# P times V by half tiles of keys in four arrays of TensorE, with the scores of another pair between its two halves

## Chip and metric

The kernel runs on one core of a Trainium2 chip. The metric is the device time of one execution in microseconds. Five engines appear in the profile: TensorE (PE; its weight loads stand apart as PEld), VectorE (DVE), ScalarE (ACT), GpSimd (POOL) and SyncE (SP), whose queue issues the transfers.

## What is computed

Windowed causal attention with a linear bias, followed by a gated MLP whose gate mixes positions. There are 8 batches of 8 heads, 576 positions, head dimension 64; the MLP is 512 to 1024 to 512. In short:

```python
scores = scale * np.matmul(q, k.transpose(0, 1, 3, 2))
mask = (rel >= 0) & (rel < 128)                 # a query sees itself and 127 keys before it
scores = np.where(mask, scores + bias[None], -1000000000.0)
attn = softmax(scores)
x = np.matmul(attn, v)                          # heads joined: (8, 576, 512)
h = np.maximum(x @ w_in, 0.0)
u, v = (h[..., :512], h[..., 512:])
v_n = (v - mean(v)) / np.sqrt(var(v) + 1e-06)
v_s = np.einsum('ts,bsd->btd', w_spatial, v_n) + b_spatial[None, :, None]
out = (u * v_s) @ w_out
```

## The kernel before

Attention works on pairs of heads. A tile holds the 64 dims of the one head in partitions 0-63 and those of the other in 64-127. The 576 queries are cut into nine blocks of 64 (`NB`), and a block of queries i meets at most the key blocks i-2, i-1 and i, so that its scores are 64, 128 or 192 columns wide (`WIDTH`). The first batch runs by a path of its own (`raw_tile`, `raw_sums`, `raw_out`); for the 28 pairs of the other batches the stages are these:

- `products` (L620, matmul L632): the scores, f32 matmuls that take 64 dims by 64 columns. For odd blocks the two heads swap partitions (`j ^ odd`), so that even blocks use two of the four 64x64 arrays and odd blocks the other two. They go block 0, 1, ... 8.
- `softmax` (L636): VectorE adds the bias and takes the maximum (L645), ScalarE takes the exponential with a sum (L651).
- `scores` (L661): scaling, and a split into a high and a low f16 plane in `pq` (ScalarE L685, VectorE L690). Two transposing transfers bring it to `pts`, keys in partitions (L696): one for even blocks, one for odd.
- `attention` (L701): v is scaled and split into f16 `vh` and `vl`; then P times V (L751). A matmul takes all 128 keys of a tile and 64 dims of a head (`j`), and streams a window of one, two or four blocks of queries (`WINDOWS`). Each window is done three times: vh with the high plane, vh with the low one, vl with the high one. Blocks of a window that do not use some of the keys meet zeros. The results stand in two PSUM banks (`xps`, queries 0 to 255 and 256 to 575), from where ScalarE (L766) and VectorE (L770) bring them to `xt`.
- `gated` (L799): the MLP of a batch, with units v (L822, and L844 for the last 64 positions), u (L874), spatial mixing (L895) and output (L921), all on the full 128x128 array. A layer norm follows every v unit; its power -0.5 is one GpSimd instruction (L792).

`clear` (L597) zeroes `pq` once, by one GpSimd memset behind the first batch's path.

The order of the instructions on each engine is set by a planner (`Plan`): every step has an engine, a cost and a due time, and a list scheduler simulates the engines and emits the steps in the order in which they begin there. The costs of the attention steps are set by hand: `SCORES`, `VALUES`, and `BOTH` for the step in which P times V of one pair is followed at once by the scores of the pair two further on ("glued", 22 of the 28). The first six pairs have their scores alone, and six pairs (the first four and the last two) their values alone.

Of the kernel before, what the change touches and what calls it, by code (L numbers as in the profile page):

```python
# [12 lines left out]
F16 = mybir.dt.float16  # L13
# [179 lines left out]
def attn_gmlp_kernel(ctx, tc, qk, v, w_in, w_spT, b_sp, w_out, outT):  # L193
# [3 lines left out]
    nc = tc.nc  # L197
    B, H, D, _, S = qk.shape
    P = 2 * D
    NP = H // 2  # L200
# [7 lines left out]
    PSC = 4096.0  # L208
    VORDER = (0, 4, 1, 2, 3)
    W = 3 * D  # L210
    QSPLIT = 2 * P
    NB = S // D

    SWITCH = 190
    SCORES, VALUES, BOTH = 1760, 1670, 3230


    WOUT = (2, 4, 6, 8)
# [8 lines left out]
    VDUE = 8000  # L227

    const = ctx.enter_context(tc.tile_pool(name="const", bufs=1))
    work = ctx.enter_context(tc.tile_pool(name="work", bufs=2))  # L230
    ps = ctx.enter_context(tc.tile_pool(name="ps", bufs=1, space=PSUM))
    ctx.enter_context(tc.manual_schedule())
    plan = Plan()
# [6 lines left out]
    def fixed(shape, dtype, name):  # L240
        t = const.tile(shape, dtype, name=name)
        return Buf(lambda: t)

    def dve(n, fast=False):
        return 75 + n / (1.92 if fast else 0.96)
# [20 lines left out]
    r1 = fixed([P, S], F32R, "r1")  # L266
    r2 = fixed([P, S], F32R, "r2")
    l2 = fixed([P, DH], F32R, "l2")
    BLOCKS = [*range(0, NB, 2), *range(1, NB, 2)]
    EVENS = (NB + 1) // 2  # L270
    WIDTH = [min(i + 1, 3) * D for i in BLOCKS]
    prob = fixed([P, sum(WIDTH)], F32, "prob")
    PLANE = [2 * EVENS * P - P, 2 * (NB - EVENS) * P - P]
    BASE = [0, 2 * PLANE[0]]
    pq = fixed([P, 2 * sum(PLANE)], F16, "pq")
    stat = [fixed([P, 4, NB], F32, f"stat{i}") for i in range(2)]

    rstat = fixed([P, 2, 4, 2 * NP], F32, "rstat")
# [3 lines left out]
    def parts(b, a, z, step=P, key=()):  # L282

        return [(b, (*key, k)) for k in range(a // step, -(-z // step))]
# [309 lines left out]
            tail(xt, due + 1200)  # L594

    def clear():
        plan.add("POOL", 2500, 0, lambda: nc.gpsimd.memset(pq(), 0.0), (), parts(pq, 0, 2 * sum(PLANE), 64))  # L597


    WINDOWS = (((0, 4, 0, 0), (1, 2, 0, 128)),  # L600
               ((1, 2, 1, 0), (2, 4, 0, 0), (3, 2, 0, 128), (3, 1, 1, 256), (4, 1, 0, 256)))


    def places(k):
        i = BLOCKS[k]
        bank, c0 = ((0, 3 * P), (2, 3 * P), (0, 0), (2, 0), (0, W), (2, W), (1, 0), (3, 0), (1, W))[i]
        odd = i % 2
        return i, odd, bank, c0, sum(WIDTH[:k]), BASE[odd] + (0 if i < 2 else P + (i // 2 - 1) * 2 * P + odd * D), WIDTH[k]

    def queries(pts, j, a, kt, n, s):  # L610

        x = [BASE[o] + a * PLANE[o] + 2 * kt * P + s * P + (j ^ o) * D for o in range(2)]
        flat = pts().rearrange("p a b -> p (a b)")
        if n == 1:
            return flat[:, x[0]:x[0] + D]
        ap = flat[:, x[0]:x[0] + D]
        steps = [[x[1] - x[0], 2], [1, D]]
        return bass.AP(ap.tensor, ap.offset, [ap.ap[0], [P, 2], *steps] if n == 4 else [ap.ap[0], *steps])

    def products(raw):  # L620

        RAWS = [(raw, t) for t in range(NQ)]
        sc = [plan.buf(ps, "s", 4, [P, 512], F32) for _ in range(4)]
        flat = lambda k: sc[k]().rearrange("p a b -> p (a b)")

        def f():
            order = sorted(range(NB), key=lambda k: (BLOCKS[k] // 2, BLOCKS[k]))
            for k in order:
                i, odd, bank, c0, _, _, n = places(k)
                for j in range(2):  # L630
                    rows = slice((j ^ odd) * D, ((j ^ odd) + 1) * D)
                    nc.tensor.matmul(flat(bank)[rows, c0:c0 + n], raw()[j * D:(j + 1) * D, 0, i * D:(i + 1) * D],  # L632
                                     raw()[j * D:(j + 1) * D, 1, (i + 1) * D - n:(i + 1) * D], start=True, stop=True, skip_group_check=True)
        return f, RAWS, [(x, 0) for x in sc], flat

    def softmax(p, due, st, sc, flat):  # L636

        SM, NM, RC, TM = range(4)
        for k in range(NB):
            i, odd, bank, c0, pc, _, n = places(k)  # L640
            pt = lambda pc=pc, n=n: prob()[:, pc:pc + n]
            d = due - 4500 + k * 350

            def f(bank=bank, c0=c0, n=n, pt=pt, odd=odd, k=k):
                nc.vector.tensor_tensor_reduce(pt(), flat(bank)[:, c0:c0 + n], tabs()[:, 2 * p + odd, W - n:], -0.125, 3e38, ALU.add, ALU.min,  # L645
                                               st()[:, NM, k:k + 1])
            cols = parts(prob, pc, pc + n, 64)
            plan.add("DVE", dve(n), d, f, [sc[bank], (tabs, 2 * p + odd)], cols + [(st, (NM, k))])

            def f(pt=pt, k=k):  # L650
                nc.scalar.activation(pt(), pt(), AF.Exp, bias=st()[:, NM, k:k + 1], scale=-1.0, accum_out=st()[:, SM, k:k + 1])  # L651
            plan.add("ACT", act(n, 2), d, f, cols + [(st, (NM, k))], cols + [(st, (SM, k))])
# [8 lines left out]
    def scores(b, p, vr, SC):  # L661

        due = when(b, p)
        st = stat[p % 2]
        SM, NM, RC, TM = range(4)
        VRS = [(vr, t) for t in range(NQ)]
        softmax(p, due, st, *SC)
        pts = plan.buf(work, "pt", 2, [P, 32, P], F16)
        for j in range(2):
            d = due + j * 1500  # L670
            ks = range(EVENS) if j == 0 else range(EVENS, NB)
            kk = slice(ks[0], ks[-1] + 1)

            def f(kk=kk):
                nc.vector.tensor_scalar(st()[:, TM, kk], st()[:, SM, kk], 1.0 / PSC, 1e-9 / PSC, ALU.mult, ALU.add)
            plan.add("DVE", 100, d, f, [(st, (SM, k)) for k in ks], [(st, (TM, j))])

            def f(kk=kk):
                nc.vector.reciprocal(st()[:, RC, kk], st()[:, TM, kk])
            plan.add("DVE", 120, d, f, [(st, (TM, j))], [(st, (RC, j))])  # L680
            for m, k in enumerate(ks):
                _, _, _, _, pc, qc, n = places(k)

                def f(n=n, pc=pc, qc=qc, k=k):
                    nc.scalar.activation(pq()[:, qc:qc + n], prob()[:, pc:pc + n], AF.Copy, scale=st()[:, RC, k:k + 1])  # L685
                cols, out = parts(prob, pc, pc + n, 64), [parts(pq, qc + a * PLANE[j], qc + a * PLANE[j] + n, 64) for a in range(2)]
                plan.add("ACT", act(n, 1), d + 100 + m * 250, f, cols + [(st, (RC, j))], out[0])

                def f(n=n, pc=pc, qc=qc, k=k, j=j):
                    nc.vector.scalar_tensor_tensor(pq()[:, qc + PLANE[j]:qc + PLANE[j] + n], prob()[:, pc:pc + n], st()[:, RC, k:k + 1],  # L690
                                                   pq()[:, qc:qc + n], ALU.mult, ALU.subtract)
                plan.add("DVE", dve(n) + 55, d + 110 + m * 250, f, cols + [(st, (RC, j))] + out[0], out[1])
            c0, n = BASE[j], 2 * PLANE[j]

            def f(c0=c0, n=n):
                nc.sync.dma_start_transpose(out=pts()[:, c0 // P:(c0 + n) // P, :], in_=pq()[:, c0:c0 + n])  # L696
            plan.add("SP", 3000, d + 1500, f, parts(pq, c0, c0 + n, 64), [(pts, j)], lag=1000)

        return lambda after: attention(p, due, vr, VRS, pts, after)

    def attention(p, due, vr, VRS, pts, after):  # L701

        vh, vl = (plan.buf(work, tag, 2, [P, NQ, P], F16) for tag in ("vh", "vl"))
        am = plan.buf(work, "am", 2, [P, 8], F32)
        d = due - 8000

        def f():
            nc.scalar.activation(vl(), vr(), AF.Abs, accum_out=am()[:, 0:1])
# [33 lines left out]
        xt = plan.buf(work, "xt", 6, [P, 2 * S + R], F32R)  # L742
        xps = [plan.buf(ps, "x", 2, [P, 512], F32) for _ in range(2)]

        def f():
            for hf, xp in enumerate(xps):
                seen = set()
                for kt, n, s, x0 in WINDOWS[hf]:
                    for l, a in ((vh, 0), (vh, 1), (vl, 0)):
                        for j in range(2):  # L750
                            nc.tensor.matmul(xp()[j * D:(j + 1) * D, x0:x0 + n * D], l()[:, kt, j * D:(j + 1) * D],  # L751
                                             queries(pts, j, a, kt, n, s), start=j not in seen, stop=False, skip_group_check=True)
                            seen.add(j)
        more, reads, writes = after or (None, [], [])

        def both(f=f, more=more):
            f()
            if more:
                more()
        plan.add("PE", BOTH if more else VALUES, due + VDUE, both, [(vh, 0), (vl, 0)] + [(pts, j) for j in range(2)] + reads, [(xp, 0) for xp in xps] + writes)  # L760
        for hf, xp in enumerate(xps):
            q0, q1 = (0, QSPLIT) if hf == 0 else (QSPLIT, S)
            n = q1 - q0
# [262 lines left out]
```

## Time and profile before

| | us |
|---|---|
| median of 3 runs | 589.46 |
| lowest, highest | 588.82, 589.75 |
| the profiled execution, its time | 586.58 |
| its span in the trace | 584.4 |

The profile is that of one execution. Its first part gives the busy time of each engine; other views give the busy time by stretches of the span, the instructions in order of time, and the chain of waits, which goes back from the last instruction to what released it. Records of TensorE overlap, since matmuls are pipelined: distances between starts tell what a matmul costs, its own duration does not.

### The profile page before, as it was taken

What the parts mean: (1) busy time and instruction counts of PE and PEld (TensorE: products, weight loads), DVE (VectorE), ACT (ScalarE), POOL (GpSimd) and SP (SyncE); (2) the same over time, 40 slices, a digit from 0 to 9 for tenths busy, and PEclk for the clock granted to TensorE, in tenths of its full rate; (3) what the DMA queues carried; (4) which work ended last, traced back from release to release, by engine and by line L of the source; (5) the groups of instructions that cost most, each with busy time, mean ns of one, the idle gap of its engine ahead of it and who ended that gap; (6) DMA issues with size and microseconds to landing.
All of it is one profiled execution on the core that took longest, in us unless ns stands there. A gap on an engine that the chain in (4) does not pass through costs nothing.

```text
span 584.4 us, 14820 instructions
## 1 busy us (share of the span) xinstructions
PE 563.7 (96%) x5448; PEld 507.4 (87%) x5448; DVE 462.5 (79%) x1747; ACT 417.2 (71%) x1312; POOL 32.3 (6%) x50
## 2 busy tenths in 40 slices
PE   4899789999999999999999999999999999999997
PEld 2466589987899989998999989998999989998997
DVE  8989999998998897878978797878977798625311
ACT  6789787999798777856877777856977777624321
POOL 1000210001000010001000010000100010001000
PEclk9999999999999999999999999999999999999999
DMA  8906347987669646676268656676278334410001
GB/s 273 343 27 235 103 84 157 205 197 151 156 140 209 171 114 140 150 177 134 71 145 180 153 123 138 144 170 144 61 131 207 100 73 76 86 51 22 1 31 51
DMA packets 144108, 77.80 MB, mean 133 GB/s; under 512 B 123426, under 2 KB 134690, under 8 KB 144036
## 3 DMA queue, kind: packets, MB, share of 16 engines
q1 hardware_dynamic: 144036, 76.87, 54.9%
q8 instruction: 42, 0.69, 0.5%
q14 instruction: 30, 0.25, 0.1%
HBM read 37.13 MB, written 9.44 MB: 80 GB/s over the span
## 4 chain that ended last, share of the span: by engine, by line
PE 82%; DVE 13%; ACT 2%; DMA 1%; issue 1%; POOL 1%; SPq 0%; ACTq 0%; POOLq 0%
PE m L895 21%; PE m L874 17%; PE m L921 17%; PE m L822 12%; PE x L751 6%; PE s L632 6%; PE m L844 2%; DVE pq L690 1%; DVE vt L796 1%; DVE st L783 1%; DMA qkraw<-in_qk_dram 1%; DVE gs L385 1%; DVE win L397 1%; DVE prob L645 1%; ACT prob L651 1%
## 5 line engine op out<-in xcount | busy, mean ns | idle before, releaser
L895 PE MATMUL m<-wsp,vn 128*128 128x288 f32 x768 | 119.7, 296 | 0.0
L651 ACT ACTIVATE prob<-prob,stat 128x192 f32<-128x192 f32 (+2 forms) x252 | 107.4, 428 | 13.1 <-DVE stat L645 12.8
L874 PE MATMUL m<-xt,win 128*128 128x288 f32 x768 | 108.8, 297 | 2.7 <-DVE vt L853 1.7
L874 PEld LDWEIGHTS m<-xt,win 128*128 128x128 f32 x768 | 104.0, 188 | 6.0 <-DVE vt L853 2.0
L895 PEld LDWEIGHTS m<-wsp,vn 128*128 128x128 f32 x768 | 107.2, 188 | 2.0 <-DVE stat L645 1.1
L921 PE MATMUL m<-gs,wout 128*128 128x288 f32 x768 | 106.1, 297 | 0.3 <-ACT o L353 0.3
L921 PEld LDWEIGHTS m<-gs,wout 128*128 128x128 f32 x768 | 102.6, 188 | 3.1 <-DVE stat L645 1.4
L685 ACT ACTIVATE pq<-prob,stat 128x192 f16<-128x192 f32 (+2 forms) x252 | 90.9, 426 | 9.0 <-ACT pq L685 5.3
L822 PE MATMUL m<-win,xt 128*128 128x512 f32 x384 | 93.8, 396 | 0.3 <-DVE vt L358 0.2
L690 DVE SCALAR_TENSOR_TENSOR pq<-prob,stat,pq 128x192 f16<-128x192 f32 (+2 forms) x252 | 87.5, 388 | 3.6 <-ACT pq L685 2.9
L822 PEld LDWEIGHTS m<-win,xt 128*128 128x128 f32 x384 | 70.8, 188 | 18.2 <-DVE st L783 0.8
L645 DVE CUSTOM_DVE_ANT_0 prob<-s,tabs 128x192 f32<-128x192 f32 (+2 forms) x252 | 71.6, 328 | 12.2 <-PE s L632 12.0
L903 DVE TENSOR_TENSOR u<-m,u 128x288 f32<-128x288 f32 x64 | 29.0, 453 | 35.7 <-PE m L895 35.3
L792 POOL TENSOR_TENSOR st<-st,nhalf 128x1 f32<-128x1 f32 (+1 forms) x40 | 26.6, 666 | 508.8 <-DVE st L788 378.1
L353 ACT CAST gs<-u 128x288 fp32r<-128x288 f32 x51 | 21.8, 428 | 41.0 <-DVE u L903 40.9
L651 ACT ACTIVATION_READ_ACCUMULATOR prob<-prob,stat 128x1 f32 x252 | 47.7, 189 | 0.0
L632 PE MATMUL s<-qkraw 64*64 64x192 f32 (+2 forms) x1008 | 45.8, 311 | 0.0
L751 PE MATMUL x<-pt,vh 128*64 128x128 f16 (+2 forms) x784 | 42.1, 229 | 0.3 <-DVE xt L770 0.3
L909 DVE TENSOR_TENSOR gs<-u,gs 128x288 fp32r<-128x288 f32 x64 | 28.9, 453 | 13.4 <-ACT gs L353 13.3
L783 DVE BATCH_NORM_STATS2 st<-vt 128x6 f32<-128x512 f32 (+1 forms) x40 | 27.5, 687 | 14.8 <-ACT vt L357 14.8
L751 PEld LDWEIGHTS <-vh 128*64 128x64 f16 x784 | 33.3, 110 | 6.1 <-issue 5.2
L632 PEld LDWEIGHTS s<-qkraw 64*64 64x64 f32 x1008 | 35.4, 133 | 2.6 <-issue 1.0
(132 smaller groups left out, 751.2 us busy)
## 6 DMA issues: line engine op xcount, KB each, us to landing
qkraw<-in_qk_dram SPq DMA_DIRECT2D x28, 576.0 KB, 4.5
out_dram<-o SPq DMA_DIRECT2D x64, 144.0 KB, 2.0
vraw<-in_v_dram SPq DMA_DIRECT2D x28, 320.0 KB, 3.7
vn<-in_w_in_dram SPq DMA_DIRECT2D x4, 512.0 KB, 7.2
wout<-in_w_in_dram SPq DMA_DIRECT2D x4, 512.0 KB, 6.3
wout<-in_w_out_dram SPq DMA_DIRECT2D x4, 512.0 KB, 3.6
gs<-in_w_spT_dram SPq DMA_DIRECT2D x4, 288.0 KB, 6.1
qkraw<-in_qk_dram SPq DMA_DIRECT2D x3, 320.0 KB, 8.2
```

The costliest lines, as they stand in the source:

```text
L632: nc.tensor.matmul(flat(bank)[rows, c0:c0 + n], raw()[j * D:(j + 1) * D, 0, i * D:(i + 1) * D], raw()[j * D:(j + 1) * D, 1, (i + 1) * D - ...
L645: nc.vector.tensor_tensor_reduce(pt(), flat(bank)[:, c0:c0 + n], tabs()[:, 2 * p + odd, W - n:], -0.125, 3e38, ALU.add, ALU.min, st()[:, N ...
L651: nc.scalar.activation(pt(), pt(), AF.Exp, bias=st()[:, NM, k:k + 1], scale=-1.0, accum_out=st()[:, SM, k:k + 1])
L685: nc.scalar.activation(pq()[:, qc:qc + n], prob()[:, pc:pc + n], AF.Copy, scale=st()[:, RC, k:k + 1])
L690: nc.vector.scalar_tensor_tensor(pq()[:, qc + PLANE[j]:qc + PLANE[j] + n], prob()[:, pc:pc + n], st()[:, RC, k:k + 1], pq()[:, qc:qc + n], ...
L751: nc.tensor.matmul(xp()[j * D:(j + 1) * D, x0:x0 + n * D], l()[:, kt, j * D:(j + 1) * D], queries(pts, j, a, kt, n, s), start=j not in see ...
L783: nc.vector.bn_stats(st()[:m, 0:6], vt()[:m])
L822: nc.tensor.matmul(pt(), xt[c]()[:, X0[a] + t * P:X0[a] + (t + 1) * P], win()[:, c, w, DH:DF], start=(n == 0), stop=(n == 3 * NC_ - 1))
L874: nc.tensor.matmul(pt()[:, :HS], win()[:, c, w, d * P:(d + 1) * P], xt[c]()[:, X0[a] + hf * HS:X0[a] + (hf + 1) * HS], start=(n == 0), sto ...
L895: nc.tensor.matmul(pt()[:, :HS], l, r, start=(n == 0), stop=(n == len(ops) - 1))
L903: nc.vector.tensor_tensor(u(), pt()[:, :HS], u(), ALU.mult)
L921: nc.tensor.matmul(pt()[:, :HS], wout[d]()[:, w, e * P:(e + 1) * P], gs[d]()[:, a, :], start=(n == 0), stop=(n == 3 * ND - 1))
```

## The change

P times V is done by half tiles: 64 keys (key block kb, in the partitions that kb's parity gives) by 64 dims, so that a matmul uses one of the four 64x64 arrays. A key block kb serves the queries kb, kb+1 and kb+2. The nine blocks of queries are split into the first five and the last four (`GROUPS`) in place of even and odd; the heads swap partitions in the first five. Each group has a PSUM bank of its own. `TURNS` pairs a key block of the one group in partitions 0-63 with one of the other group in partitions 64-127. There are two phases; in the second the two groups change sides. Between them stand a GpSimd memset of an unused column of `am`, which waits for the last matmul of the first phase and for which the first one of the second phase waits, and, in a glued step, the scores of the other pair. The scores go in the order 2, 5, 3, 6, 4, 7, 0, 8, 1. `pq` has four planes of seven tiles, and only four gaps in each half have to be zero; two VectorE memsets do that.

```diff
-    SCORES, VALUES, BOTH = 1760, 1670, 3230
+    SCORES, VALUES, BOTH = 1600, 1800, 2760
...
-    BLOCKS = [*range(0, NB, 2), *range(1, NB, 2)]
-    EVENS = (NB + 1) // 2
+    FIRSTS = (NB + 1) // 2
+    GROUPS = (range(FIRSTS), range(FIRSTS, NB))
+    QSPLIT = FIRSTS * D
...
-        plan.add("POOL", 2500, 0, lambda: nc.gpsimd.memset(pq(), 0.0), (), parts(pq, 0, 2 * sum(PLANE), 64))
+        for half, (a, z) in enumerate(((D, 6 * P + D), (0, 6 * P + D))):
+            gaps = [2 * half * PLANE + k * PLANE + x for k in range(2) for x in (a, z)]
+            def f(gaps=gaps, step=z - a):
+                ap = pq()[:, gaps[0]:gaps[0] + D]
+                nc.vector.memset(bass.AP(ap.tensor, ap.offset, [ap.ap[0], [PLANE, 2], [step, 2], [1, D]]), 0.0)
+            plan.add("DVE", dve(4 * D, True), 0, f, (), [x for g in gaps for x in parts(pq, g, g + D, 64)])
...
-    WINDOWS = (((0, 4, 0, 0), (1, 2, 0, 128)),
-               ((1, 2, 1, 0), (2, 4, 0, 0), (3, 2, 0, 128), (3, 1, 1, 256), (4, 1, 0, 256)))
+    def values(half, kb):
+        return [i for i in (kb, kb + 1, kb + 2) if i in GROUPS[half]]
+    TURNS = (((0, 0), (1, 5)), ((0, 2), (1, 7)), ((0, 4), (1, 3))), (((1, 6), (0, 1)), ((1, 4), (0, 3)), ((1, 8), None))
...
-            order = sorted(range(NB), key=lambda k: (BLOCKS[k] // 2, BLOCKS[k]))
-            for k in order:
+            for i in (2, 5, 3, 6, 4, 7, 0, 8, 1):
...
+        def phase(turns):
+            flat, done = pts().rearrange("p a b -> p (a b)"), []
+            for turn in turns:
+                for l, a in ((vh, 0), (vh, 1), (vl, 0)):
+                    for half, kb in [x for x in turn if x]:
+                        rows = slice(kb % 2 * D, kb % 2 * D + D)
+                        ks = values(half, kb)
...
                         for j in range(2):
-                            nc.tensor.matmul(xp()[j * D:(j + 1) * D, x0:x0 + n * D], l()[:, kt, j * D:(j + 1) * D],
-                                             queries(pts, j, a, kt, n, s), start=j not in seen, stop=False, skip_group_check=True)
...
+                            done.append(nc.tensor.matmul(xps[half]()[j * D:(j + 1) * D, x0:x0 + len(ks) * D], l()[rows, kb // 2, j * D:(j + 1) * D], ap,
+                                             start=(half, j) not in seen, stop=False, skip_group_check=True))
...
+            last, _ = phase(TURNS[0])
+            turn = nc.gpsimd.memset(am()[:, 7:8], 0.0)
             if more:
                 more()
+            _, first = phase(TURNS[1])
+            for x, y in ((turn, last), (first, turn)):
+                tc.add_manual_dep(x.ins, y.ins.name, mybir.DependencyInfo(mybir.DependencyClass.Sync, mybir.DependencyReason.DATA), reason="turn")
```

On TensorE, a glued step before ends its values (x from pt and vh or vl) and has the scores (s from qkraw) behind them; the next unit (m) follows:

```order
L751 LDWEIGHTS vl
L751 MATMUL x_71<-pt,vl 64x64
L632 MATMUL s_66<-qkraw 64x64 x2
L632 MATMUL s_68<-qkraw 64x128 x2
L632 MATMUL s_66<-qkraw 64x192 x2
L632 MATMUL s_68<-qkraw 64x192 x2
L632 MATMUL s_66<-qkraw 64x192 x2
L632 MATMUL s_68<-qkraw 64x192 x2
L632 MATMUL s_67<-qkraw 64x192 x2
L632 MATMUL s_69<-qkraw 64x192 x2
L632 MATMUL s_67<-qkraw 64x192 x2
L921 MATMUL m<-gs,wout_857 128x288 x3
```

The same place in the changed kernel, from the last matmul of the first phase to the first of the second:

```order
L758 MATMUL x_71<-pt,vl 64x64
L629 MATMUL s_67<-qkraw 64x192 x2
L629 MATMUL s_66<-qkraw 64x192 x2
L629 MATMUL s_69<-qkraw 64x192 x2
L629 MATMUL s_66<-qkraw 64x192 x2
L629 MATMUL s_69<-qkraw 64x192 x2
L629 MATMUL s_68<-qkraw 64x192 x2
L629 MATMUL s_67<-qkraw 64x64 x2
L629 MATMUL s_68<-qkraw 64x192 x2
L629 MATMUL s_67<-qkraw 64x128 x2
L758 LDWEIGHTS vh
L758 MATMUL x_71<-pt,vh 64x192
```

The scores have moved from behind the values into their middle, and the narrow blocks 0 and 1 from the front of the scores to their end. A step has 66 values matmuls where it had 42. Among TensorE's units the third glued step of a batch stands one spatial unit later than before, and the last glued step of the kernel four u units earlier; the rest of the steady order is as it was.

On GpSimd, from the first layer norm on (st and nhalf: the power of a layer norm), the queue before:

```order
L792 TENSOR_TENSOR st<-st,nhalf 128x1 x3
L597 MEMSET pq 128x4096
L792 TENSOR_TENSOR st<-st,nhalf 128x1
L792 TENSOR_TENSOR st<-st,nhalf 64x1
L792 TENSOR_TENSOR st<-st,nhalf 128x1
L792 TENSOR_TENSOR st<-st,nhalf 64x1
L792 TENSOR_TENSOR st<-st,nhalf 128x1 x4
```

And in the changed kernel:

```order
L805 TENSOR_TENSOR st<-st,nhalf 128x1 x4
L805 TENSOR_TENSOR st<-st,nhalf 64x1
L767 MEMSET am 128x1 x4
L805 TENSOR_TENSOR st<-st,nhalf 128x1
L805 TENSOR_TENSOR st<-st,nhalf 64x1
L805 TENSOR_TENSOR st<-st,nhalf 128x1
L767 MEMSET am 128x1
L805 TENSOR_TENSOR st<-st,nhalf 128x1 x2
L767 MEMSET am 128x1 x3
L805 TENSOR_TENSOR st<-st,nhalf 128x1
L767 MEMSET am 128x1
L805 TENSOR_TENSOR st<-st,nhalf 64x1
```

The wide memset of pq is gone from this queue, and 28 small ones (one per pair) stand between the powers. In the steady batches, from the last three rows on, one power stands ahead of the first memset of a batch and the other four behind it.

## Rows read from the trace of the kernel before

**Rows 1.** The page's first part: busy time of each engine, share of the span.

```profile
PE 563.7 (96%) x5448; PEld 507.4 (87%) x5448; DVE 462.5 (79%) x1747; ACT 417.2 (71%) x1312; POOL 32.3 (6%) x50
```

**Rows 2.** Stretches: length, PE, PEld, DVE, ACT, POOL busy, clock, DMA share, GB/s.

```profile
0.00:77.30 77.30, 61.91 (x524) 39.89 (x524) 71.56 (x264) 61.31 (x191) 9.06 (x14) 1.00 0.56 187
77.30:117.30 40.00, 39.96 (x401) 38.02 (x401) 38.22 (x147) 34.77 (x113) 1.14 (x1) 1.00 0.77 161
117.30:152.70 35.40, 33.67 (x364) 27.91 (x363) 32.21 (x125) 29.94 (x93) 3.74 (x5) 1.00 0.74 167
152.70:584.40 431.70, 428.15 (x4162) 401.57 (x4162) 320.49 (x1213) 291.22 (x916) 18.39 (x30) 1.00 0.52 118
```

**Rows 3.** The same view for the scores' line L632 alone (PE, PEld).

```profile
152.70:584.40 431.70, 34.32 (x756) 26.52 (x756) 1.00 0.52 118
```

**Rows 4.** The chain around one glued step: start, duration, engine, tile, line.

```profile
302.03 1.84 PE m L895 x14
...
305.45 1.47 PE x L751 x42
306.92 1.56 PE s L632 x32
308.48 2.06 PE m L895 x14
```

**Rows 5.** Timeline of TensorE in that step: start, duration of the group, line.

```profile
305.38 0.41 PE L751 MATMUL x<-pt,vh 128*64 128x256 f16 x4
305.62 0.28 PE L751 MATMUL x<-pt,vl 128*64 128x256 f16 x2
305.73 0.28 PE L751 MATMUL x<-pt,vh 128*64 128x128 f16 x4
...
305.90 0.28 PE L751 MATMUL x<-pt,vh 128*64 128x128 f16 x4
...
306.56 0.23 PE L751 MATMUL x<-pt,vh 128*64 128x64 f16 x4
...
306.72 0.20 PE L751 MATMUL x<-pt,vl 128*64 128x64 f16 x2
306.85 1.63 PE L632 MATMUL s<-qkraw 64*64 64x64 f32 x36
```

**Rows 6.** GpSimd: its timeline, the powers of L792 together, the chain around one.

```profile
0.41 0.10 POOL L1014 MEMSET const-uint8-127<- 128x1 uint8 x1
...
271.11 0.72 POOL L792 TENSOR_TENSOR st<-st,nhalf 128x1 f32<-128x1 f32 x1 [51.61 <-DVE st L788]
...
L792 POOL TENSOR_TENSOR st<-st,nhalf x40: 541/548/1508, 35.3 to 542.8; 128x1 f32<-128x1 f32 x32, 64x1 f32<-64x1 f32 x8
...
46.19 1.02 POOL st L792
47.22 0.03 issue
```

**Rows 7.** The chain at three other steps, and one pair's transposes on SyncE's queue.

```profile
273.26 1.47 PE x L751 x42
...
490.33 1.47 PE x L751 x42
...
520.79 6.57 PE m L921 x48
...
466.34 4.72 SPq L696 DMA_TRANSPOSE pt<-pq  x2
```

**Rows 8.** Timeline of VectorE and GpSimd in the opening; L796 together (min/median/max).

```profile
64.52 0.16 DVE L675 TENSOR_SCALAR stat<-stat 128x4 f32<-128x4 f32 x1
64.59 3.85 DVE L796 TENSOR_SCALAR vt<-vt,st 128x512 f32<-128x512 f32 x1
64.65 3.52 POOL L597 MEMSET pq<- 128x4096 f16 x1 [1.34 <-PE x L583]
...
L796 DVE TENSOR_SCALAR vt<-vt,st x40: 521/540/3852, 35.9 to 543.7; 128x512 f32<-128x512 f32 x32, 64x512 f32<-64x512 f32 x8
```

More of the change, by code (lines that the diff above doesn't have):

```diff
@@ L210, in attn_gmlp_kernel @@
     W = 3 * D
-    QSPLIT = 2 * P
     NB = S // D
     SWITCH = 190
-    SCORES, VALUES, BOTH = 1760, 1670, 3230
+    SCORES, VALUES, BOTH = 1600, 1800, 2760
     WOUT = (2, 4, 6, 8)
@@ L268, in attn_gmlp_kernel @@
     l2 = fixed([P, DH], F32R, "l2")
-    BLOCKS = [*range(0, NB, 2), *range(1, NB, 2)]
-    EVENS = (NB + 1) // 2
-    WIDTH = [min(i + 1, 3) * D for i in BLOCKS]
+    FIRSTS = (NB + 1) // 2
+    GROUPS = (range(FIRSTS), range(FIRSTS, NB))
+    QSPLIT = FIRSTS * D
+    WIDTH = [min(i + 1, 3) * D for i in range(NB)]
     prob = fixed([P, sum(WIDTH)], F32, "prob")
-    PLANE = [2 * EVENS * P - P, 2 * (NB - EVENS) * P - P]
-    BASE = [0, 2 * PLANE[0]]
-    pq = fixed([P, 2 * sum(PLANE)], F16, "pq")
+    PLANE = 7 * P
+    pq = fixed([P, 4 * P * NP * 2], F16, "pq")
     stat = [fixed([P, 4, NB], F32, f"stat{i}") for i in range(2)]
@@ L596, in clear, with places @@
     def clear():
-        plan.add("POOL", 2500, 0, lambda: nc.gpsimd.memset(pq(), 0.0), (), parts(pq, 0, 2 * sum(PLANE), 64))
-    WINDOWS = (((0, 4, 0, 0), (1, 2, 0, 128)),
-               ((1, 2, 1, 0), (2, 4, 0, 0), (3, 2, 0, 128), (3, 1, 1, 256), (4, 1, 0, 256)))
[L604 to L618, printed above, removed]
+        for half, (a, z) in enumerate(((D, 6 * P + D), (0, 6 * P + D))):
[4 more added lines that the diff above has]
+            plan.add("DVE", dve(4 * D, True), 0, f, (), [x for g in gaps for x in parts(pq, g, g + D, 64)])
+    def places(i):
+        half = int(i >= FIRSTS)
+        bank, c0 = ((1, 0), (1, D), (1, W), (3, 0), (3, W), (0, 0), (0, W), (2, 0), (2, W))[i]
+        first = (0, P, 2 * P, 2 * P + W, 4 * P + P)[i] if half == 0 else (D, 2 * P, 2 * P + W, 4 * P + P)[i - FIRSTS]
+        return half, 1 - half, bank, c0, sum(WIDTH[:i]), 2 * half * PLANE + first, WIDTH[i]
+    def values(half, kb):
+        return [i for i in (kb, kb + 1, kb + 2) if i in GROUPS[half]]
+    TURNS = (((0, 0), (1, 5)), ((0, 2), (1, 7)), ((0, 4), (1, 3))), (((1, 6), (0, 1)), ((1, 4), (0, 3)), ((1, 8), None))
     def products(raw):
@@ L626, in f @@
         def f():
-            order = sorted(range(NB), key=lambda k: (BLOCKS[k] // 2, BLOCKS[k]))
-            for k in order:
-                i, odd, bank, c0, _, _, n = places(k)
+            for i in (2, 5, 3, 6, 4, 7, 0, 8, 1):
+                _, odd, bank, c0, _, _, n = places(i)
                 for j in range(2):
@@ L639, in softmax @@
         for k in range(NB):
-            i, odd, bank, c0, pc, _, n = places(k)
+            _, odd, bank, c0, pc, _, n = places(k)
             pt = lambda pc=pc, n=n: prob()[:, pc:pc + n]
@@ L667, in scores @@
         softmax(p, due, st, *SC)
-        pts = plan.buf(work, "pt", 2, [P, 32, P], F16)
+        pts = plan.buf(work, "pt", 2, [P, 4 * PLANE // P, P], F16)
         for j in range(2):
             d = due + j * 1500
-            ks = range(EVENS) if j == 0 else range(EVENS, NB)
+            ks = GROUPS[j]
             kk = slice(ks[0], ks[-1] + 1)
@@ L685, in f @@
                     nc.scalar.activation(pq()[:, qc:qc + n], prob()[:, pc:pc + n], AF.Copy, scale=st()[:, RC, k:k + 1])
-                cols, out = parts(prob, pc, pc + n, 64), [parts(pq, qc + a * PLANE[j], qc + a * PLANE[j] + n, 64) for a in range(2)]
+                cols, out = parts(prob, pc, pc + n, 64), [parts(pq, qc + a * PLANE, qc + a * PLANE + n, 64) for a in range(2)]
                 plan.add("ACT", act(n, 1), d + 100 + m * 250, f, cols + [(st, (RC, j))], out[0])
                 def f(n=n, pc=pc, qc=qc, k=k, j=j):
-                    nc.vector.scalar_tensor_tensor(pq()[:, qc + PLANE[j]:qc + PLANE[j] + n], prob()[:, pc:pc + n], st()[:, RC, k:k + 1],
+                    nc.vector.scalar_tensor_tensor(pq()[:, qc + PLANE:qc + PLANE + n], prob()[:, pc:pc + n], st()[:, RC, k:k + 1],
                                                    pq()[:, qc:qc + n], ALU.mult, ALU.subtract)
                 plan.add("DVE", dve(n) + 55, d + 110 + m * 250, f, cols + [(st, (RC, j))] + out[0], out[1])
-            c0, n = BASE[j], 2 * PLANE[j]
+            c0, n = 2 * j * PLANE, 2 * PLANE
             def f(c0=c0, n=n):
@@ L743, in attention @@
         xps = [plan.buf(ps, "x", 2, [P, 512], F32) for _ in range(2)]
-        def f():
[L746 to L750, printed above, removed]
-                            nc.tensor.matmul(xp()[j * D:(j + 1) * D, x0:x0 + n * D], l()[:, kt, j * D:(j + 1) * D],
-                                             queries(pts, j, a, kt, n, s), start=j not in seen, stop=False, skip_group_check=True)
-                            seen.add(j)
@@ L754, in attention @@
-        more, reads, writes = after or (None, [], [])
-        def both(f=f, more=more):
-            f()
+        seen = set()
+        def phase(turns):
[5 more added lines that the diff above has]
+                        ks = values(half, kb)
+                        at = places(ks[0])[5] + a * PLANE + (kb - max(0, ks[0] - 2)) * D
+                        x0 = (ks[0] - GROUPS[half][0]) * D
+                        for j in range(2):
+                            c = at // P * P + (j ^ (1 - half)) * D
+                            ap = flat[rows, c:c + D]
+                            if len(ks) > 1:
+                                ap = bass.AP(ap.tensor, ap.offset, [ap.ap[0], [P, len(ks)], [1, D]])
+                            done.append(nc.tensor.matmul(xps[half]()[j * D:(j + 1) * D, x0:x0 + len(ks) * D], l()[rows, kb // 2, j * D:(j + 1) * D], ap,
+                                             start=(half, j) not in seen, stop=False, skip_group_check=True))
+                            seen.add((half, j))
+            return done[-1], done[0]
@@ L758, in both @@
+        more, reads, writes = after or (None, [], [])
+        def f():
+            last, _ = phase(TURNS[0])
+            turn = nc.gpsimd.memset(am()[:, 7:8], 0.0)
             if more:
                 more()
-        plan.add("PE", BOTH if more else VALUES, due + VDUE, both, [(vh, 0), (vl, 0)] + [(pts, j) for j in range(2)] + reads, [(xp, 0) for xp in xps] + writes)
+            _, first = phase(TURNS[1])
+            for x, y in ((turn, last), (first, turn)):
+                tc.add_manual_dep(x.ins, y.ins.name, mybir.DependencyInfo(mybir.DependencyClass.Sync, mybir.DependencyReason.DATA), reason="turn")
@@ L761, in attention @@
+        plan.add("PE", BOTH if after else VALUES, due + VDUE, f, [(vh, 0), (vl, 0)] + [(pts, j) for j in range(2)] + reads, [(xp, 0) for xp in xps] + writes)
         for hf, xp in enumerate(xps):
```

## The prediction

> **What bounds the kernel now.** I read the summary first: TensorE is busy for 563.7 of 584.4 us, VectorE for 462.5 [rows 1]. A share of the whole says little here, so the next view is busy time by stretch [rows 2]. It shows three regimes. Up to 77.3 us, while inputs and weights are being prepared, VectorE is the full one (71.56 of 77.30) and TensorE is not (61.91). From 117.3 to 152.7 VectorE and ScalarE carry 32.21 and 29.94 of 35.40 and the chain of waits runs over them. In the rest TensorE has no holes: 39.96 of 40.00, then 428.15 of 431.70 us, with VectorE at 320.49. There a TensorE nanosecond removed is a nanosecond off the end. The view of the scores' line by stretch counts 756 records in that last stretch [rows 3]; 36 make a step, so 21 of the 22 glued steps lie there, and behind them the last two values steps, alone.
>
> The chain shows what one glued step costs: values 1.47, scores 1.56, 3.03 us [rows 4]. The rows around it show the price of a change of array shape. Fourteen matmuls on the full array take 1.84 behind a unit of their own kind and 2.06 behind the scores.
>
> **Values, per column.** TensorE's timeline gives starts [rows 5]. One pair of matmuls (two dims halves side by side) that streams 256 columns takes 305.73 - 305.62 = 0.11 us; three pairs of 128 take 0.17 (0.057 each); five pairs of 64 take 0.16 (0.032 each). Before, each of three passes (vh, vh, vl) has two windows of 256, three of 128, two of 64: 3 x (0.220 + 0.171 + 0.064) = 1.365 us, as the trace has it (305.38 to 306.75). The window pads: 16 blocks of 64 for all 128 keys, where only 24 half-key blocks are wanted, which is 12 of full depth. After, keys 0-63 and 64-127 of a tile stream in different rows of the array, side by side. A turn costs its longer half: 192, 192, 64 columns before the scores and 192, 128, 64 behind them. With 0.084 for 192 (between the prices of 128 and 256): 3 x (0.084 + 0.084 + 0.032) + 3 x (0.084 + 0.057 + 0.032) = 0.600 + 0.519 = 1.12 us. **Term: -0.25 per step.** It rests on four arrays running at once in f16. No row shows that for f16; the scores, 64x64 in f32, do it: they stream 832 columns in the even blocks' arrays and 704 in the odd ones' beside them, within 1.56 us.
>
> **Scores.** With evens on one pair of arrays and odds on the other the longer queue has 832 columns; blocks 0-4 against 5-8 give 768 and 768. The 1.56 us, less the 0.10 of a change of shape (next term), give 1.46/832 = 1.75 ns per column, so **-0.11 per step**, glued or alone.
>
> **Shape changes.** Before: full to 128x64, to 64x64, to full. The inner one costs 306.85 - 306.75 = 0.10. After: full to 64x64, and back; values and scores have the same shape, but alternate f16 and f32. No row shows that seam. Bounds: none, as between two units of one shape, or 0.10 at both seams. I take none, because the shape is what changes in every row with a gap, and add 0.03 for the first weights of the second half (the first two pairs take 0.24 where two take 0.22). **Term: -0.07**, bounds -0.10 and +0.13.
>
> **One glued step:** -0.25 - 0.11 - 0.07 = -0.43 us; bounds -0.23 and -0.50. The 21 in the dense stretch give **-9.0**. The 22nd lies in the VectorE-bound stretch and counts nothing.
>
> **The turn.** The two halves write each other's PSUM bank from other rows, so the second waits until a GpSimd memset has seen the first done. Its path: the last 64-wide matmul's record (0.20) [rows 5], 0.03 to GpSimd (as the handoff behind the row at 46.19), the memset (0.10), 0.03 back: some 0.38 us with a little for a busy queue [rows 6]. In a glued step some 1.35 us of scores cover it; if that cover went, it would cost 0.35. GpSimd works in order, so what stands ahead of the memset counts: one layer norm's power instruction, which in the rows at 271.11 ends at 271.83, before the values start at 273.26 [rows 6, 7]; the other four stand behind the memset now. Behind the waiting TensorE stands all its later work.
>
> **Values alone:** six, without scores to cover the turn: -0.25 + 0.03 + 0.35 = +0.13 each, bounds 0 and +1.4 (the longest GpSimd row of this size is 1.51 against 0.10). Four lie in dense stretches: **+0.5**. Scores alone: three in the dense 40 us: **-0.3**.
>
> **The opening.** The chain holds one odd row: a VectorE normalisation of 3.85 us (median 0.54), beside the one GpSimd memset that clears 4,096 columns in 3.52 [rows 8]. VectorE is the bound there, and nothing else explains the row. The change clears only the gaps, by two short VectorE memsets (some 0.16 each, as the short row at 64.52). Saved: 3.3 - 0.3; but the first memset waits, on VectorE itself, for the same opening matmuls that the GpSimd one waited for. **Term: -2.5**, bounds -3.2 and 0 (TensorE, at 61.9 of 77.3, or another order of the opening takes over).
>
> **Priced at nothing.** VectorE and ScalarE keep their instructions; only the split of the 576 queries moves (320 + 256). The first x half is complete one second half later; after the fourth pair of a batch 6.57 us of output matmuls cover it [rows 7]; without them the next unit would wait for that half's 0.5 us. Block 0, which VectorE takes first, now comes near the end of the scores, so a softmax may start some 1.3 us later; VectorE has 111 us to spare in the dense stretch [rows 2], and where it has none this would cost up to 1.3 us in each of three steps. The transposes shrink from 32 to 28 tiles and are issued 15 us or more ahead (466.34 for the values at 490.33) [rows 7]. That also covers the last glued step, which moves four units earlier.
>
> **Sum:** -9.0 + 0.5 - 0.3 - 2.5 = -11.3 us. The profiled execution took 586.58 us (span 584.4), so it becomes 575.3; the median of the runs, 589.46, stands 2.9 above it, so the forecast is **578.2 us**.
>
> **Rivals.** (1) *The halves of the array do not overlap in f16.* Then a turn costs both: 3 x (0.168 + 0.141 + 0.064) + 3 x (0.168 + 0.114 + 0.032) = 2.06, +0.70 for values; the glued step is +0.52: 21 x 0.52 + 4 x 1.08 - 0.3 - 2.5 = +12.4, **602 us**. Against it: the scores. It decides once the two row halves lose about half of their overlap (25 steps x 0.94 x 0.48 = 11.3). Chance 0.04.
> (2) *Matmuls cost per instruction.* There are 66 instead of 42 per step. The densest row here starts ten in 0.16 us, 16 ns each, which gives 1.06 us and would not bind; the mean before, 1.34/42 = 32 ns, would give 2.1, as in (1). Against it: 64-wide pairs cost a third of 256-wide ones, so columns are what is paid. Chance 0.04, time 580 to 602.
> The Trainium skill, "TensorE: Matmul & The Clock Gate", section "Wait — 56ns, not 53.3ns?", states that starts never come closer than about 25 ns. By it 66 would take an estimated 1.65 us and the run would end near 592; the 16 ns above already contradict it.
> (3) *The turn comes late.* If VectorE holds the small memset up as some row held the power of 1.51 us, the turn takes 1.8: 0.45 past the scores. That eats the glued gain, and the lone steps add 4 x 1.5: 589.46 + 6.1 - 2.8, **593 us**. It decides from 1.8 us. Against it: 548 ns is the median of the 40 rows, so long ones are few. Chance 0.05.
> The Trainium skill, "SBUF — State Buffer", section "Who interferes with whom", says that GpSimd is fully blocked by a VectorE instruction in a two-port mode until that ends; the row of 3.85 is the same lock from the other side.
> (4) *The small end:* both seams keep 0.10 and the opening gives nothing: 21 x -0.23 + 0.2 = -4.6, **585 us**; if TensorE also waits for something moved, 588. Chance 0.12.
>
> **How the numbers follow.** Forecast 0.75, with 574.5 (every bound good: -0.50 x 22 - 3.2 - 0.3 = -14.5, and 0.5 for the scatter of the runs, 588.82 to 589.75) to 584.5. Rival (4) widens it to **574.5 to 585.5**; what lies outside is some 0.18. 0.2% (1.2 us) is about what measurement can tell. Faster: 0.75 + 0.09 + 0.01 = 0.85. Same: 0.05, from (4) and (3). Slower: 0.10.
>
> **What would show it.** Right: glued steps of about 2.6 us from one full-array unit to the next; batches some 1.7 us shorter than 66.1; lone values of 1.6; no VectorE row of 3.8 us near 65 us and the first dense stretch 2 to 3 us earlier. Wrong: a hole on TensorE ahead of the second half, released by GpSimd (3); starts of the two halves one after the other (1); a gap at f16 to f32 (4); VectorE or ScalarE as releaser of TensorE after 150 us.

## The result

| | before | changed |
|---|---|---|
| median of 4 runs, us | 589.14 | 575.32 |
| lowest, highest | 588.46, 589.75 | 574.67, 575.71 |
| the profiled execution, its span | 586.58, 584.4 | 575.71, 574.0 |

The changed kernel takes 0.9765 of the time (95% interval 0.9748 to 0.9782), 13.8 us less where 11.3 were forecast. The two profiled executions stand only 10.9 apart: that of before was faster than all four runs in the table, that of the changed kernel is the slowest of its four.

The first part of the page of the changed kernel, busy time by engine (against [rows 1]):

```profile
PE 553.5 (96%) x6120; PEld 504.4 (88%) x6120; DVE 459.8 (80%) x1750; ACT 414.5 (72%) x1311; POOL 33.2 (6%) x77
```

TensorE lost 10.2 us of busy time though it has 672 matmuls more (28 steps, 66 instead of 42 in each), and is still the full engine. By stretch, with the columns of [rows 2]:

```profile
0.00:77.30 77.30, 63.67 (x519) 41.24 (x520) 68.12 (x276) 62.86 (x200) 3.93 (x12) 0.93 0.62 193
...
152.70:574.00 421.30, 417.36 (x4711) 396.81 (x4709) 320.34 (x1214) 288.59 (x915) 24.77 (x55) 1.00 0.49 114
```

The last stretch stays dense on TensorE: 417.36 of 421.30. In the opening VectorE has 68.12 where it had 71.56, and the granted clock is 0.93 where it was 1.00.

The chain of waits of the changed kernel around a glued step and a lone one (start, duration, engine, tile, line; against [rows 4] and [rows 7]):

```profile
302.79 0.67 PE x L758 x30
...
303.49 1.34 PE s L629 x30
304.83 0.51 PE x L758 x30
305.34 6.55 PE m L934 x48
...
509.17 0.75 PE x L758 x26
509.92 0.03 POOLq L767
509.95 0.07 issue
510.01 0.11 POOL am L767
510.12 0.04 issue
510.17 0.69 PE x L758 x30
510.86 6.55 PE m L934 x48
```

From the start of the values to the next unit the glued step takes 305.34 - 302.79 = 2.55 us, before 3.03: **-0.48**. The second half of the values begins where the scores end; GpSimd isn't in the chain. In the lone step it is: 1.69 us from 509.17 to 510.86. The same step before takes 1.47:

```profile
519.33 1.47 PE x L751 x42
```

The small memset by its line, in the changed kernel:

```profile
L767 POOL MEMSET am<- x28: 98/98/103, 108.1 to 510.0; 128x1 f32 x28
...
who waited for it (us, times):
...
  PE x L758: 1.7, 6
```

Of its 28 executions six made TensorE wait, as many as there are lone steps.

A second execution of the changed kernel gives TensorE's timeline of a glued step by starts, with the groups of [rows 5]:

```profile
300.35 0.36 PE L758 MATMUL x<-pt,vh 64*64 64x192 f16 x8
300.54 0.25 PE L758 MATMUL x<-pt,vl 64*64 64x192 f16 x4
300.62 0.33 PE L758 MATMUL x<-pt,vh 64*64 64x192 f16 x8
300.74 0.29 PE L758 MATMUL x<-pt,vl 64*64 64x128 f16 x4
300.80 0.23 PE L758 MATMUL x<-pt,vh 64*64 64x64 f16 x4
300.86 0.20 PE L758 MATMUL x<-pt,vl 64*64 64x64 f16 x2
300.87 0.23 PE L758 MATMUL x<-pt,vh 64*64 64x64 f16 x4
300.91 0.39 PE L629 MATMUL s<-qkraw 64*64 64x192 f32 x2
300.93 0.20 PE L758 MATMUL x<-pt,vl 64*64 64x64 f16 x2
300.96 1.50 PE L629 MATMUL s<-qkraw 64*64 64x192 f32 x34
302.27 0.36 PE L758 MATMUL x<-pt,vh 64*64 64x192 f16 x8
...
302.90 0.54 PE L934 MATMUL m<-gs,wout 128*128 128x288 f32 x2
```

By these starts the values take (300.91 - 300.35) + (302.90 - 302.27) = 1.19 us where they took 1.47, and the scores 302.27 - 300.91 = 1.36 where they took 1.56. One change of shape is in either time of the values: before it is the gap of 0.10 ahead of the scores, now the change to the full array behind the second half. The first two matmuls of the scores start at 300.91, ahead of the last two of the values at 300.93: the seam from f16 to f32 has no gap.

**Where the gain lies.** The first glued step of the dense stretch starts here in the traces of before and of the changed kernel:

```profile
161.26 0.41 PE L751 MATMUL x<-pt,vh 128*64 128x256 f16 x4
```

```profile
161.12 0.36 PE L758 MATMUL x<-pt,vh 64*64 64x192 f16 x8
```

In a second execution of each it starts here:

```profile
162.86 0.41 PE L751 MATMUL x<-pt,vh 128*64 128x256 f16 x4
```

```profile
158.75 0.36 PE L758 MATMUL x<-pt,vh 64*64 64x192 f16 x8
```

The second spans are 586.0 and 571.7. From that step to the end before takes 423.14 us in both executions, the changed kernel 412.88 and 412.95. So the dense stretch gives **-10.2**, repeatable to 0.1: 21 x -0.48 + 2 x 0.22 = -9.6 in the steps (in the chains every one of the 21 takes 3.03 before and 2.55 now), and 0.6 outside them. Of this 0.4 lies behind the last output copy, which ends 3.07 us ahead of the end before (581.33) and 2.63 in the changed kernel (571.37); why was not traced. What comes ahead of the dense stretch varies between executions of one program by 1.6 and 2.4 us, and the two pairs differ widely: the first gives -0.1 (161.12 - 161.26), the second -4.1. By the medians it gives -13.8 + 10.2 = **-3.6**, a difference and not a reading.

### The profile page after: what moved, and what is told of

Same layout as the page of the kernel before. It is cut to its first block, busy times and chain, and to the rows that moved or that the text cites. A ratio compares the mean times of both kernels' runs of the same rounds, so it can differ in the third digit from the quotient of the medians.

```text
span 574.0 us, 16254 instructions
## 1 busy us (share of the span) xinstructions
PE 553.5 (96%) x6120; PEld 504.4 (88%) x6120; DVE 459.8 (80%) x1750; ACT 414.5 (72%) x1311; POOL 33.2 (6%) x77
## 4 chain that ended last, share of the span: by engine, by line
PE 72%; ACT 0%; issue 0%; POOL 0%; POOLq 0%; ACTq 0%
PE m L908 18%; PE m L934 16%; PE m L887 14%; PE m L835 12%; PE s L629 5%; PE x L758 5%; PE m L857 2%; ACT prob L648 0%; ACT o L352 0%; ACT u L356 0%; POOL am L767 0%; POOLq L767 0%; ACTq L352 0%
## 5 line engine op out<-in xcount | busy, mean ns | idle before, releaser
L642 DVE CUSTOM_DVE_ANT_0 prob<-s,tabs 128x192 f32<-128x192 f32 (+2 forms) x252 | 70.1, 330 | 3.8 <-PE s L629 3.4
L648 ACT ACTIVATION_READ_ACCUMULATOR prob<-prob,stat 128x1 f32 x252 | 48.9, 194 | 0.0
L629 PE MATMUL s<-qkraw 64*64 64x192 f32 (+1 forms) x1008 | 43.5, 310 | 0.0
L758 PEld LDWEIGHTS <-vh 64*64 64x64 f16 x1232 | 34.8, 107 | 7.9 <-issue 5.2
L805 POOL TENSOR_TENSOR st<-st,nhalf 128x1 f32<-128x1 f32 (+1 forms) x40 | 28.2, 705 | 224.9 <-DVE st L801 189.3
L758 PE MATMUL x<-pt,vh 64*64 64x192 f16 (+2 forms) x1232 | 39.6, 224 | 1.7 <-POOL am L767 1.7
L779 ACT ACTIVATE xt<-x,am 128x320 fp32r<-128x320 f32 (+1 forms) x56 | 25.2, 495 | 20.4 <-PE x L758 20.4
L796 DVE BATCH_NORM_STATS2 st<-vt 128x6 f32<-128x512 f32 (+1 forms) x40 | 27.4, 688 | 14.6 <-ACT vt L356 14.5
```

Source lines behind the costliest of these rows:

```text
L758: done.append(nc.tensor.matmul(xps[half]()[j * D:(j + 1) * D, x0:x0 + len(ks) * D], l()[rows, kb // 2, j * D:(j + 1) * D], ap, start=(half ...
L805: nc.gpsimd.tensor_tensor(st()[:m, 11:12], st()[:m, 10:11], nhalf()[:m], ALU.pow)
```

## Experiments on the turn and the arrays

**Scores behind the values.** The changed kernel with its scores after both halves, so that nothing covers the turn:

```diff
             turn = nc.gpsimd.memset(am()[:, 7:8], 0.0)
+            _, first = phase(TURNS[1])
             if more:
                 more()
-            _, first = phase(TURNS[1])
```

> The changed kernel with the scores of a glued step behind both phases of its values instead of between them. Theory (the scores cover the turn): the lone values steps of the changed kernel take 1.65 to 1.71 us and its lone scores 1.46, so a step is about 1.67 + 1.46 less 0.09 for a change of shape that does not occur = 3.04 us, against 2.55 with the scores between: 21 x 0.49 = +10.3 us, near 585.5. TensorE waits for GpSimd in every step. Rival (the place of the scores matters little, the gain is the columns alone): within 2 us of 575.3.

Measured: 585.56 us, beside 587.96 for before on the same chip; ratio 0.9959 (0.9945 to 0.9973). The chain around one glued step of this kernel:

```profile
291.22 0.75 PE x L758 x26
...
292.08 0.11 POOL am L767
...
292.23 0.66 PE x L758 x28
...
292.93 1.34 PE s L629 x30
294.27 1.78 PE m L887 x12
```

and who waits for the memset, from its view of waits (us in total, times, longest):

```profile
PE x L758 <- POOL am L767: 8.6, 28, 0.4
```

The step takes 294.27 - 291.22 = 3.05 us, 0.50 more than in the changed kernel, and all 28 steps wait where six did. An uncovered turn therefore costs 0.50 and not the 0.35 of the prediction; 21 of them are 10.5 us, and the times differ by (0.9959 - 0.9765) x 589.14 = 11.4. Without the place of the scores most of the gain would be gone.

**A longer turn.** Five more memsets of the same column ahead of the second half:

```diff
-            turn = nc.gpsimd.memset(am()[:, 7:8], 0.0)
+            begin = nc.gpsimd.memset(am()[:, 7:8], 0.0)
+            for _ in range(5):
+                turn = nc.gpsimd.memset(am()[:, 7:8], 0.0)
...
-            for x, y in ((turn, last), (first, turn)):
+            for x, y in ((begin, last), (first, turn)):
```

> The changed kernel with five more small GpSimd memsets in a row in each turn, each waiting for the one before, some 0.65 us in all. Theory (the scores cover the turn of a glued step, 1.34 us against a turn of 0.4): glued steps stay at 2.55 us; the lone values steps grow by 0.65, four of them in dense stretches: +2.6 us over the changed kernel, ratio 0.981. Rival (the turn is on the path in every step): +0.65 x 28 = +18 us.

Measured: 578.32, ratio 0.9826 (0.9804 to 0.9848), which is (0.9826 - 0.9765) x 589.14 = 3.6 us above the changed kernel. The chain of this kernel in a glued and in a lone step:

```profile
303.32 0.67 PE x L758 x30
...
305.37 0.51 PE x L758 x30
305.87 6.55 PE m L936 x48
...
510.47 0.75 PE x L758 x26
...
512.04 0.11 POOL am L769
...
512.89 3.14 PE m L936 x22
```

The glued step is again 305.87 - 303.32 = 2.55. The lone one takes 512.89 - 510.47 = 2.42, 0.73 more; four in dense stretches are 2.9 us. The scores have room for a turn that costs a lone step 0.73 us more; only the lone steps pay.

**Halves of the array apart.** The turns of the changed kernel have one key block each, so that the two row halves follow one another:

```diff
-    TURNS = (((0, 0), (1, 5)), ((0, 2), (1, 7)), ((0, 4), (1, 3))), (((1, 6), (0, 1)), ((1, 4), (0, 3)), ((1, 8), None))
+    TURNS = (((0, 0), None), ((0, 2), None), ((0, 4), None), ((1, 5), None), ((1, 7), None), ((1, 3), None)), (((1, 6), None), ((1, 4), None), ((1, 8), None), ((0, 1), None), ((0, 3), None))
```

> The changed kernel with each phase doing first all its key blocks in partitions 0-63 and then all those in 64-127, so that neighbours in the program use the same rows of the array. Theory (halves overlap only when they are neighbours, matmuls issue in order): a values step costs both halves, 2.06 instead of 1.12 us: 25 x 0.94 = +23 us, near 599. Rival (each array takes its own matmuls from far ahead in the queue): within 2 us of 575.3.

Measured: 589.97, ratio 1.0034 (1.0018 to 1.0051), between the two expectations. Its chain around one glued step:

```profile
293.60 0.98 PE x L758 x26
...
296.00 0.76 PE x L758 x25
296.77 1.78 PE m L887 x12
```

The step takes 296.77 - 293.60 = 3.17, 0.62 more than with paired turns, where the prediction's prices gave 0.94. That is also 0.14 more than before, so the overlap is what the change lives on, and it needs partners that stand next to each other in the program. The price was too high for a half alone: the first phase streams 3 x 832 columns in 0.98 us, 0.39 ns each, and I had priced it at 1.12. What of the rest is overlap where one half's matmuls end and the other's begin was not told apart.

**Scores between the halves in the kernel before.** There the scores move between the two banks of the values, and nothing else changes:

```diff
-        def f():
-            for hf, xp in enumerate(xps):
+        def f(hf):
+            xp = xps[hf]
...
         def both(f=f, more=more):
-            f()
+            f(0)
             if more:
                 more()
+            f(1)
```

> The kernel before with the scores of a glued step between the windows of the first and of the second PSUM bank; nothing else. Theory (a change of the array's shape costs 0.10 us): two seams instead of one, so +0.10 to +0.2 per step, 22 steps: +2 to +4.4 us over the kernel before, 591 to 593.5. Rival (the place of the scores is itself worth something, through an earlier softmax): below the kernel before.

Measured: 590.53, ratio 1.0043 (1.0027 to 1.0059). The chain of one step:

```profile
295.07 0.62 PE x L752 x12
295.68 1.56 PE s L632 x32
297.25 0.97 PE x L752 x30
298.22 1.78 PE m L876 x12
```

298.22 - 295.07 = 3.15 against 3.03. With values in 128x64 and scores in 64x64 the new place adds a change of shape, 0.12 us, close to the 0.10 read at the one seam of before. So the gain isn't the place by itself: the place is free only since values and scores share a shape.

**Narrow blocks first.** The changed kernel with its scores in another order:

```diff
-            for i in (2, 5, 3, 6, 4, 7, 0, 8, 1):
+            for i in (0, 5, 1, 6, 2, 7, 3, 8, 4):
```

> The changed kernel with the scores in the order 0, 5, 1, 6, 2, 7, 3, 8, 4: the same 768 columns for each pair of arrays, but the narrow blocks first. Theory (the balance 768 to 768 is what the scores gain, each array runs its own queue): glued steps of 2.55 +- 0.03 us, within 1 us of 575.3. Rival (the order matters, since a narrow block beside a wide one holds up the queue): steps longer by 0.05 to 0.1 us, +1 to +3 us.

Measured: 574.40, ratio 0.9765 (0.9737 to 0.9794); the glued step is 2.55 us again. Which block goes first does not count, and no softmax that starts later or earlier shows in the time. Both orders split the columns into 768 and 768, so this run does not test the split; what it gives is seen where scores stand alone, in 86.28 - 84.82 = 1.46 us in the changed kernel where they took 1.56.

**More steps glued.** Two more in the stretch that VectorE bounds, 24 instead of 22:

```diff
-    APART = 4
+    APART = 2
```

> The changed kernel with APART 2: the values of the third and fourth pair are glued to scores too, so that four values steps stand alone instead of six, and four scores. In TensorE's time two steps of 1.67 + 1.46 become 2.55 each: -1.2 us if TensorE is the bound there. Theory (VectorE and ScalarE are the bound between 115 and 150 us, where these steps lie): within 1 us of the changed kernel, ratio 0.9765 +- 0.0017. Rival: -1.2 us, ratio 0.9745.

Measured: 576.20, ratio 0.9793 (0.9772 to 0.9813), 1.6 us above the changed kernel, where the intervals still touch. That is above the band of the theory and further from the rival's 0.9745. Four steps wait for a turn instead of six, and the time is no better: less of TensorE's time there did not bring the end forward.

## Experiments on the opening

**The wide memset on VectorE.** The kernel before, with `clear` at its place in the plan but issued on the other engine; the orders of the other engines stay:

```diff
-        plan.add("POOL", 2500, 0, lambda: nc.gpsimd.memset(pq(), 0.0), (), parts(pq, 0, 2 * sum(PLANE), 64))
+        plan.add("POOL", 2500, 0, lambda: nc.vector.memset(pq(), 0.0), (), parts(pq, 0, 2 * sum(PLANE), 64))
```

> The kernel before with the one clearing memset of pq on VectorE instead of GpSimd, at the same place of the program; TensorE's, ScalarE's and SyncE's orders are unchanged. Theory (the wide GpSimd memset holds VectorE up for 3.3 us while VectorE is the bound of the opening): the row of 3.85 us falls to about 0.55, a VectorE memset of 1 to 1.5 us comes in, the end moves by -1.8 to -2.3 us against the kernel before. Rival (the opening has slack, or loses it again before the dense stretch): within 0.7 us of the kernel before.

Measured: 586.21, beside 588.22 for before; ratio 0.9962 (0.9947 to 0.9978), by the ratio -2.2 us. Its VectorE timeline and the normalisation's line (min/median/max):

```profile
66.77 1.76 DVE L597 MEMSET pq<- 128x2048 uint32 x1 [0.37 <-ACT xt L353]
...
L796 DVE TENSOR_SCALAR vt<-vt,st x40: 521/540/549, 37.2 to 544.2; 128x512 f32<-128x512 f32 x32, 64x512 f32<-64x512 f32 x8
```

The row of 3.85 [rows 8] is gone and the longest is 0.549, so the GpSimd memset made it. The kernel is faster though VectorE now does the 1.76 us of clearing itself. It need not be the normalisation that is held up: in the run with the scores between the halves the same memset (67.62, for 3.52) meets another row of VectorE, of a line that takes 0.42 elsewhere in the opening:

```profile
67.78 3.64 DVE L377 TENSOR_SCALAR vraw<-vraw 128x512 f32<-128x512 f32 x1 [0.76 <-ACT vraw L373]
```

**The wide memset put back.** The changed kernel with one GpSimd memset over all of `pq`; the planner orders the opening anew:

```diff
-        for half, (a, z) in enumerate(((D, 6 * P + D), (0, 6 * P + D))):
...
-            plan.add("DVE", dve(4 * D, True), 0, f, (), [x for g in gaps for x in parts(pq, g, g + D, 64)])
+        plan.add("POOL", 2500, 0, lambda: nc.gpsimd.memset(pq(), 0.0), (), parts(pq, 0, 4 * PLANE, 64))
```

> The changed kernel with the one wide GpSimd memset that clears all of pq, in place of the two short VectorE memsets of the gaps; the planner sets a somewhat different order in the opening. Theory (as above): +2.5 to +3 us over the changed kernel, a ratio to the kernel before of 0.981. Rival (the opening's slack): the changed kernel's ratio of 0.9765 within 0.001.

Measured: 579.62, ratio 0.9847 (0.9824 to 0.9869), (0.9847 - 0.9765) x 589.14 = 4.8 us above the changed kernel, more than expected. Rows of its GpSimd and VectorE timelines:

```profile
67.88 3.52 POOL L597 MEMSET pq<- 128x4096 f16 x1 [1.81 <-ACT xt L352]
...
68.24 3.43 DVE L803 TENSOR_SCALAR vt<-vt,st 128x512 f32<-128x512 f32 x1
```

The long row is back: 3.43 us beside a memset of 3.52. The surplus over its 2.9 us belongs to an opening in another order; the two can't be told apart in this run.

**Both kernels once more**, unchanged, for a second trace of each:

> The kernel before, unchanged, profiled once more, to see how far its opening differs from one execution to the next: the first profiled execution was 2.6 us shorter than the median of the other runs, the changed kernel's was not. Theory (the opening's granted clock and the place where the wide GpSimd memset meets VectorE vary): the dense stretch from the values step near 207 us to the end is the same 377 us within 0.2 us, and what differs lies ahead of it, with a granted clock below 1.00 in some of the first 80 us. Rival (the dense stretch itself varies): it differs by over 1 us.

> The changed kernel, unchanged, profiled once more. Theory: glued steps of 2.55 us and the stretch from the values step near 205.4 us to the end the same 368.4 us within 0.2 us; the opening differs by up to 2 us with its granted clock. Rival: as for the kernel before.

Measured: 588.20 and 573.37. These are the second executions used above. No kernel here beats the changed one clearly. Two things were not tried: taking the turn away, which would let two row halves write one bank unordered, and giving the lone steps something else to cover their turns.

## Why the prediction was right, and where it was off

| term, us | predicted | measured |
|---|---|---|
| glued step | -0.43 (-0.23 to -0.50) | -0.48 |
| dense stretch from 161 us: glued steps and two lone values | -9.0 + 0.3 | -10.2 |
| values alone, each | +0.13 | +0.22 |
| scores alone, each | -0.11 | -0.11 |
| all ahead of 161 us | -2.5 + 0.3 - 0.3 | -3.6, by the medians |
| sum | -11.3 | -13.8 |

The time lies 0.8 us inside the good end of the range, 574.5. No two large errors cancel in it: the glued steps and the opening came out better than their middle values, and only the lone values worse.

**What bounds it:** right. TensorE is dense from the step at 161 us to the end, and no wait on VectorE or ScalarE replaced the time taken out: ScalarE waits 20.4 us for the values (L779), off the chain.

**Values:** right. Four arrays run at once in f16, as the f32 scores had suggested: in the chain the two halves of a glued step take 0.67 and 0.51, and 0.98 and 0.76 with the row halves apart. Predicted were 1.47 - 0.25 = 1.22, measured 1.19, both with one change of shape.

**Scores and seams:** right, with a remainder of 0.02 that wasn't foreseen. Together they were to give 1.56 - 0.11 - 0.07 = 1.38 and take 1.36. I held a seam of 0.10 possible as a bound; the starts at 300.91 and 300.93 show none.

**The turn:** covered in all glued steps, as forecast. Its price without cover was too low: 0.50 by the run with the scores behind, 1.69 - 1.19 = 0.50 in the lone step. The chain shows what I missed: the group of the first half counts 0.75 where a covered one counts 0.67, since its last matmul has to end; the handoff takes 0.25 (0.03, 0.07, 0.11, 0.04); and the second half takes 0.69 where behind scores it takes 0.51, which I read as a start with nothing else under way. With six lone steps, of which four count, this is 0.4 us in all.

**The opening:** the mechanism was right and the size of the term off; with the seams near their good bound this is what makes 13.8 of 11.3. The rows gave 3.85 - 0.54 - 2 x 0.16 = 3.0, and I took 2.5 off, because the first memset might wait and another engine might take over. Neither of the two memsets waits: VectorE has no idle time ahead of them (L602). Whether another engine took over can't be read, as the chain of the changed kernel can't be followed back beyond 158.55 us. By the medians -3.6 comes ahead of the first dense glued step. Moving the memset alone gave -2.2 while VectorE still spent 1.76 on it; two short ones of 0.165 spend 1.4 less, which as an estimate makes -3.6 too. That the rest is this and not the new order of the opening is argued and not shown: the run with the memset put back changes both.

**Rivals.** (1) and (2) would show in the glued step, at 3.5 us; it is 2.55. The Trainium skill, "TensorE: Matmul & The Clock Gate", section "Wait — 56ns, not 53.3ns?", would let no two matmuls start within some 25 ns. In the timeline 34 matmuls of the values start between 300.35 and 300.93, 17 ns each: for matmuls that alternate between four arrays the measurement decides against it. (3) needed a turn of 1.8 us; the memset's longest is 0.103, and even six in a row stay under the scores. (4) needed gaps at both seams. The Trainium skill, "SBUF — State Buffer", section "Who interferes with whom", was read as one lock with two sides. The runs show that VectorE is held up while the memset lasts, 3.85 against 0.549; that its row is in a two-port mode no run shows, and the records put its start 0.06 us ahead of the memset's (64.59 and 64.65), so they don't tell which came first.

## What to carry to other kernels

Cutting matmuls to the size of one array paid here only because arrays worked side by side: with the partners apart in the program the step was longer than before. If the neighbours in the program have the same shape too, another unit of that shape can be put into a pause between two halves and hides a handoff that cost 0.5 us here. When part of a kernel is bound by an engine, look there for single rows many times their median: taking one such row away was worth 2.2 us here. Set the sum against a median, and time the repeatable part of the span apart from the part that scatters.

## What the runs showed beside that

The granted clock of TensorE falls in some openings of both kernels. One microsecond in the changed kernel's profile (columns of [rows 2]):

```profile
50.00:51.00 1.00, 1.00 (x3) 0.33 (x1) 1.00 (x5) 0.55 (x2) 0.00 (x0) 0.50 0.34 61
```

and from its timeline of TensorE the matmul ahead of it:

```profile
49.05 0.54 PE L525 MATMUL s<-qkraw 64*64 64x192 f32 x4 [2.94 <-DVE rstat L534]
```

TensorE stood still for 2.94 us, waiting for VectorE; then it worked at 0.50, the lower of its two levels (1.2 GHz), until about 53 us. All seven traces of kernels with this opening have the hole (2.91 to 2.97) and the fall, which in some begins within the hole. In the four traces of kernels with the opening of before that wait is 1.23 or 1.24 long, and in the run with the memset put back no wait from 44 to 56 us is longer than 0.64; the clock stays at 1.00 there. So the changed order of the opening brings a hole and a slow stretch on TensorE which no step of the prediction held. What they cost at the end is not shown; the -3.6 is what is left after them. Other falls come in one execution and not in the next: the second one of before had 0.83 from 10 to 20 us, the first 1.00. Four executions of the kernel with the narrow blocks first go from a span of 570.8 us at a mean clock of 1.000 to 573.5 at 0.991. Times here scatter by 1 to 3 us, and the clock goes with only a part of it: on one chip ten executions of before at 0.997 have spans from 584.1 to 587.4. Profile and median can differ by as much as a term of the sum.
